# Seven half-size products for the fourth tile's second layer, with the sums of weights and one batch's copies of k moved

## The chip, the core and the metric

The kernel runs on one core of one Trainium2 chip. The core has a matrix engine (TensorE, PE in the profile, with PEld for its weight loads), a vector engine (VectorE, DVE), a scalar engine (ScalarE, ACT), GpSimd (POOL) and SyncE (SP). Each takes its instructions in the order in which they were written for it, and they wait for each other by semaphores. Here POOL and SP issue nearly all transfers. The metric is the device time of one execution in microseconds (us); the median of three runs stands for a kernel.

## The reference

Attention over 8 batches, 8 heads, 576 positions and head size 64, followed by a feed-forward network over all 4608 tokens. Heads 0 to 3 attend to the last 32 positions, heads 4 to 7 to every fourth of the last 128.

```python
scores = scale * np.matmul(q, k.transpose(0, 1, 3, 2))
scores = np.where(masks[None, :, :, :], scores, -1000000000.0)
attn = np.exp(scores - np.max(scores, axis=-1, keepdims=True))
attn = attn / (np.sum(attn, axis=-1, keepdims=True) + 1e-09)
x = np.matmul(attn, v)          # then (4608, 512): tokens by heads and head size
h = np.maximum(x @ w_in, 0.0)   # w_in 512 x 2048
out = h * h @ w_out             # w_out 2048 x 512
```

## The kernel before

**Tiles and groups.** The 4608 tokens are nine tiles of 512 (the first two are worked in halves). Each tile has 32 groups of PE work. Groups 0 to 15 are the first layer: one group makes 128 rows of h for 512 tokens, ACT applies the maximum with 0 (L1038) and DVE squares in place in `h2T` (L1041). Groups 16 to 31 are the second layer. Over the whole program the third tile has groups 64 to 95, the fourth 96 to 127, the fifth 128 to 159. A group's number sets everything: `WEIGH` and the list `steps` name groups, and after a group has been written for the engines, the work that names it follows, the sums of weights first.

**Attention between the groups.** The attention of a batch is not a stage of its own. At certain groups a *visit* puts some 100 to 140 small matmuls (L408) into PE's queue: scores of one pair of heads, and products with v and row sums of another. Before a visit, ACT makes the exponents (L773) and DVE masks them (L778) and adds where blocks overlap (L781, L790). After it ACT makes the reciprocal (L740 to L755) and DVE writes the normalised result to `xT`, the first layer's input (L758, L762), which also frees the banks of PSUM that the visit wrote. In the fourth tile the visits fall after groups 101, 111 and 119 and belong to the fifth batch; the last one also makes scores of the sixth.

**Copies.** q and k come through POOL's loads, are turned by SP's transposes into `planes`, and are copied into place on DVE: k into `kbd` by L379 (code K), the ends of the far heads' k by L390 (code R) and of q by L388 (code I).

**Two forms of the second layer.** Tiles below `FAST` use `g2`: 4 blocks of 128 tokens times 16 f, 64 matmuls of 512 columns (L1322). A block reads f in order, four to a group, so the last four f are wanted by the fourth group. From `FAST` on, the tile uses `g2_fast`: seven products in place of eight of the matrix cut in two by two (a Strassen-Winograd scheme), each 8 f times 2 blocks of tokens of 256 columns, 112 matmuls (L1282). It needs
- four sums of weights, `w_sum`, in two halves each: eight DVE operations of 128 x 1024 (`weigh`, L1438), made once. They lie in the memory that staged the third batch's q and k;
- sums of activations, `h_sum`: `add_up` (L1177) makes for each half of f four operations of 128 x 1024 out of the squared `h2T`. They lie in the memory that staged the fourth batch;
- sums of results: DVE adds products into `whole` (L1184) besides ACT's copies.

With `FAST` the first layer also runs in another order: unit u makes row block f = u // 2 + 8 (u % 2), so two units make one row block of each half of f, and DVE squares them in one operation of 2 x 512. For the last two units it squares singly.

**The order of the products** while attention still runs beside (`crowded`) is M1, half of M2, M6, the rest of M2, M5, a visit, then M7, M3, M4. M1 reads h of the first eight f for one half of the tokens, M2 of the last eight, M6 and M5 read sums.

Of the kernel before, what the change touches and what calls it, by code (L numbers as in the profile page):

```python
# [64 lines left out]
def kernel(  # L65
# [12 lines left out]
    DM, DFF = moe_w_in.shape  # L78
# [16 lines left out]
    NT = 512  # L95
    NTILES = NTOK // NT
    XB = 2
    FAST = 4
    WEIGH = (95, 95, 102, 103, 104, 118, 118, 127)
    WEIGH_IN = (18, 19, 20, 21, 22, 23, 195, 195)  # L100
    GATHER = (219, 220, 228, 232)
    PAIRED = 5
# [50 lines left out]
    HD = DM // 2  # L153
# [573 lines left out]
    def natural_step(b: int, code: str):  # L727
# [37 lines left out]
        else:  # L765
            g = int(code[2])
            second = g ^ ((b, e) in [(x, 1) for x in (NATURAL, *range(FAST + 1, B))])
            n = 384 if e >= NE // 2 else (448, 384)[g]
# [222 lines left out]
    def ffn_groups(tk0: int, nt: int):  # L991
# [3 lines left out]
        early = NT <= tk0 <= 3 * NT  # L995
        per = NT // nt
        at = tk0 // nt % per * nt
        h2 = h2T[:, :, at : at + nt]
        fast = tk0 >= FAST * NT
        kts = (2, 0, 3, 1) if tk0 > 3 * NT else (2, 3, 1, 0) if tk0 == 2 * NT else (0, 1, 2, 3) if tk0 == 0 else (2, 3, 0, 1)  # L1000
# [3 lines left out]
        over = g0 // gr != (g0 + nm - 1) // gr  # L1004
# [151 lines left out]
        sums_at = {7: (0, 4), 15: (4, 8)} if not mixed else {}  # L1156
        visited, crowded = (FAST <= tk0 // NT < x for x in (B - 1, B - 2))

# [20 lines left out]
        final = tk0 + nt == NTOK  # L1179
# [3 lines left out]
        def plus(to, one, two_):  # L1183
            nc.vector.tensor_tensor(out=to, in0=one, in1=two_, op=ALU.add)  # L1184

        def keep(m, c0, c1, n=2):

            parts = [(0, half, tk0 + RES * half), (half, half, tk0)] if over else [(0, P, tk0)]
            for x, k, row in parts:
                to = out[row : row + RES * k, :].rearrange("(p m) c -> p m c", m=RES)  # L1190
                nc.sync.dma_start(to[:, m : m + 2 * n - 1 : 2, c0:c1], whole[x : x + k, m : m + 2 * n - 1 : 2, c0:c1])

        def after(name):

            bank = {k: t[:, :, :] for k, t in cur.items()}
            if name == "M1":
                nc.scalar.copy(c11, bank["X"])
            elif crowded and name in ("M6", "M5"):
                nc.scalar.copy(c21 if name == "M6" else c12, bank["X"])
            elif crowded and name != "M2":  # L1200
                to, one, two_ = {"M7": (c22, "V", c12), "M3": (c12, "Q", c12), "M4": (c21, "V", c21)}[name]
                plus(to, bank[one], two_)
                if not over or name != "M7":
                    keep(int(name != "M3"), HD if name == "M7" else 0, HD if name == "M4" and not over else DM)
            elif name == "M5":
                nc.scalar.copy(c22, bank["Y"])
            elif name == "M6":
                nc.scalar.copy(c12, bank["X"])
                if final:
                    plus(c12, c12, c22)  # L1210
            elif name == "M3":
                plus(c12, bank["Y"], c12)
            elif name == "M7":
                plus(c22, bank["X"], c22)
                keep(1, HD, DM)
            elif name == "M2":
                plus(c11, bank["Z"], c11)
                if not crowded:
                    keep(0, 0, HD if final else DM)
            elif name == "M4":  # L1220
                nc.scalar.copy(c21, bank["X"])
                keep(1, 0, HD)
# [203 lines left out]
    def weigh(x):  # L1426

        y, f = divmod(x, 2)
        fs, gs = slice(4 * f, 4 * f + 4), slice(NF // 2 + 4 * f, NF // 2 + 4 * f + 4)
        b11, b12, b21, b22 = (w_out_sb[:, z, c : c + HD] for z in (fs, gs) for c in (0, HD))  # L1430
        to = [w[:, fs, :] for w in w_sum]
        order = (
            (to[0], b12, b11),
            (to[2], b22, b12),
            (to[1], b22, to[0]),
            (to[3], b21, to[1]),
        )
        nc.vector.tensor_tensor(out=order[y][0], in0=order[y][1], in1=order[y][2], op=ALU.subtract)  # L1438
# [79 lines left out]
    groups, steps = [], []  # L1518
# [20 lines left out]
    for b in range(NATURAL, B):  # L1539
        t = G * (b - 1)  # L1540
        early = b == NATURAL
        def visit(at, scs, pvs):
            steps.append((at, 2, b, "V0" + "/".join(",".join(f"{x}{y}" for x, y in z) for z in (scs, pvs))))
# [32 lines left out]
        else:  # L1576
            visit(t + 15, [(b, 3), (b, 1)], [(b, 0), (b, 2)][: 1 + (b >= PAIRED)])
            quick = b > FAST
            if not quick:
# [23 lines left out]
        for x, code in enumerate(("K00", "K01", "K10", "K11")):  # L1603
            if b < PAIRED:
                steps.append((start + 2 + x // 2 if early else t - 6 + x, 1, b, code))
            else:
                steps.append((t - 30 + x // 2 if b > PAIRED else t - 16 + x, 1 + 2 * (b == PAIRED), b, code + "0"))
                steps.append((t + 1 + x, 1, b, code + "1"))
        for x, code in enumerate(("Q01", "Q10")):
            if b < PAIRED:  # L1610
# [7 lines left out]
    for g, group in enumerate(groups):  # L1618
# [9 lines left out]
        group()  # L1628
        for x in [x for x in range(len(WEIGH)) if WEIGH[x] == g]:
            weigh(x)  # L1630
# [38 lines left out]
```

## Time and profile before

| What | Value |
|---|---|
| median of three runs | 286.48 us (286.25 to 286.54) |
| the profiled execution | 285.32 us |
| its span | 283.5 us |
| PE busy | 277.6 us, 98% of the span |
| DVE busy | 200.5 us, 71% |
| ACT busy | 190.9 us, 67% |
| POOL busy | 122.8 us, 43% |
| granted TensorE clock | 1.0 |

The span is the time from the first instruction to the last in the profiled execution; 1.8 us lie around it. A row of the timeline gives start and length in us from the start of the span, the engine, the line, the operation, what it writes and reads, the shapes, and how many instructions of one kind were merged. What stands in brackets is idle time of the engine ahead of the row and who ended it. A row of the chain gives start, length and what the time went to. Instructions on DVE overlap at their ends, so the distance between two starts says how long one holds the queue.

### The profile page before, as it was taken

How to read it: one execution, taken by the hardware profiler on the slowest of the kernel's cores; microseconds unless marked ns; L12 is line 12 of the kernel's file. 1: busy time of each engine (PE TensorE's matmuls, PEld its weight loads, DVE VectorE, ACT ScalarE, POOL GpSimd, SP SyncE). 2: the span in 40 equal slices, each digit the busy share in tenths (PEclk: the TensorE clock that was granted, in tenths of full speed). 3: DMA queues.
4: the chain of work that ended last, by engine and by line, in shares of the span. 5: the costliest groups of instructions: out<-in, count | busy, mean ns of one | idle time of the engine just before them, and what ended most of it. 6: DMA issues, size and time to landing. Idle time of an engine off the chain costs nothing.

```text
span 283.5 us, 8614 instructions
## 1 busy us (share of the span) xinstructions
PE 277.6 (98%) x3545; PEld 195.7 (69%) x3545; DVE 200.5 (71%) x482; ACT 190.9 (67%) x387; POOL 122.8 (43%) x208
## 2 busy tenths in 40 slices
PE   7899999999999999999999999999999999999995
PEld 6589746958755545555545787578757887899984
DVE  2686644664859766779649867987787679889752
ACT  6788726786856875697556875687568657776620
POOL 8686358663672976667285778900000000000000
PEclk9999999999999999999999999999999999999999
DMA  8999999999999999999999999910400030000314
GB/s 119 196 183 205 206 198 218 191 145 168 187 168 214 166 140 191 201 148 151 145 230 178 130 163 146 146 30 2 150 0 3 2 124 26 0 2 0 114 37 150
DMA packets 85607, 36.70 MB, mean 129 GB/s; under 512 B 53312, under 2 KB 81728, under 8 KB 85568
## 3 DMA queue, kind: packets, MB, share of 16 engines
q0 software_dynamic: 49056, 18.49, 60.4%
q1 hardware_dynamic: 36368, 17.55, 30.5%
q8 instruction: 28, 0.46, 0.7%
q14 instruction: 11, 0.09, 0.2%
q10 hardware_dynamic: 144, 0.10, 0.1%
HBM read 37.50 MB, written 9.44 MB: 166 GB/s over the span
## 4 chain that ended last, share of the span: by engine, by line
PE 93%; DMA 2%; DVE 1%; POOL 1%; issue 1%; ACT 1%; POOLq 0%
PE pf L1025 35%; PE pf L1282 22%; PE pf L1322 20%; PE pa L1077 4%; PE po L408 2%; DMA kb<-in_k_dram 2%; PE po L1077 2%; PE pf L408 2%; PE pa L408 2%; PE pd L1077 1%; PE pd L408 1%; PE pa L841 1%; DVE planes L374 1%; DVE h2T L1041 1%; PE pf L893 0%
## 5 line engine op out<-in xcount | busy, mean ns | idle before, releaser
L1025 PE MATMUL pf<-xT,w_in 128*128 128x512 bf16 (+1 forms) x608 | 107.9, 335 | 0.0
L1025 PEld LDWEIGHTS <-w_in 128*128 128x128 bf16 x608 | 67.2, 114 | 34.7 <-issue 0.3
L1038 ACT ACTIVATE h2T<-pf 128x512 bf16<-128x512 f32 x119 | 69.2, 601 | 27.0 <-PE pf L1025 26.8
L1041 DVE TENSOR_TENSOR h2T<-h2T 128x512 bf16<-128x512 bf16 (+1 forms) x95 | 45.3, 493 | 22.4 <-ACT h2T L1038 20.7
L1322 PE MATMUL pf<-w_out_sb,h2T 128*128 128x512 bf16 x256 | 57.3, 379 | 0.1
L361 POOL DMA_DIRECT2D vbd<-in_v_dram x80 | 43.1, 551 | 20.9 <-DMA qb<-in_q_dram 10.4
L1322 PEld LDWEIGHTS <-h2T 128*128 128x128 bf16 x256 | 24.3, 98 | 27.9
L1282 PEld LDWEIGHTS <-h2T 128*128 128x128 bf16 x256 | 24.5, 98 | 3.0
L1328 ACT COPY whole<-pf 128x512 f32<-128x512 f32 x14 | 8.2, 584 | 14.1 <-PE pf L1322 14.0
L755 ACT ACTIVATE rec<-rec 128x576 f32<-128x576 f32 x24 | 16.3, 692 | 0.5
L353 POOL DMA_DIRECT2D vbd<-in_v_dram x20 | 11.9, 608 | 10.3 <-DMA qb<-in_q_dram 4.5
L1184 DVE TENSOR_TENSOR whole<-pf,whole 128x512 f32<-128x512 f32 (+2 forms) x19 | 12.0, 631 | 6.2 <-PE pf L1282 5.3
L215 POOL DMA_DIRECT2D kb<-in_k_dram x19 | 13.1, 690 | 7.5 <-DMA w_in<-in_moe_w_in_dram 2.5
L237 POOL DMA_DIRECT2D vbd<-in_v_dram x16 | 11.0, 693 | 11.3 <-DMA kb<-in_k_dram 7.2
L1282 PE MATMUL pf<-w_out_sb,h2T 128*128 128x256 bf16 x128 | 15.8, 273 | 0.0
L1282 PE MATMUL pf<-kb,h2T 128*128 128x256 bf16 x128 | 15.8, 273 | 0.0
L1282 PE MATMUL pf<-qb,qb 128*128 128x256 bf16 x128 | 15.3, 273 | 0.0
L215 POOL DMA_DIRECT2D qb<-in_q_dram x19 | 13.4, 704 | 3.7 <-DMA vd<-in_v_dram 1.5
L773 ACT ACTIVATE pt<-pa 128x384 bf16<-128x384 f32 (+1 forms) x26 | 12.0, 497 | 4.0 <-DVE xT L762 3.4
L1282 PEld LDWEIGHTS <-qb 128*128 128x128 bf16 x128 | 12.5, 98 | 1.4
L347 POOL DMA_DIRECT2D vd<-in_v_dram x20 | 12.1, 617 | 1.7 <-PE pf L1025 1.0
L758 DVE TENSOR_TENSOR xT<-pf,rec 128x512 bf16<-128x512 f32 x11 | 7.6, 689 | 7.3 <-ACT rec L755 7.3
(221 smaller groups left out, 498.9 us busy)
## 6 DMA issues: line engine op xcount, KB each, us to landing
out_dram<-whole SPq DMA_DIRECT2D x21, 256.0 KB, 3.9
out_dram<-whole SPq DMA_DIRECT2D x18, 128.0 KB, 6.0
qb<-in_q_dram POOLq DMA_DIRECT2D x7, 320.0 KB, 7.6
kb<-in_k_dram POOLq DMA_DIRECT2D x7, 320.0 KB, 7.9
vd<-in_v_dram POOLq DMA_DIRECT2D x34, 64.0 KB, 6.2
w_out_sb<-in_moe_w_out_dram POOLq DMA_DIRECT2D x4, 512.0 KB, 12.8
qb<-in_q_dram POOLq DMA_DIRECT2D x6, 256.0 KB, 6.9
kb<-in_k_dram POOLq DMA_DIRECT2D x6, 256.0 KB, 7.8
```

What stands on the lines that cost most here:

```text
L215: nc.gpsimd.dma_start(t[p0 : p0 + n, part, h0:h1, :], src[b, h0:h1, t0 : t0 + RES * n, :].rearrange("h (p r) d -> p h (r d)", r=RES),)
L347: nc.gpsimd.dma_start(vds[b][rows, e, :, :], v[b, H // 2 + 2 * e + (hl ^ crossed(b, e + NE // 2)), 0:512, :].rearrange("(m p r) d -> p m ( ...
L361: nc.gpsimd.dma_start(v_rows[b % 2][p0 + 16 * r : p0 + 16 * r + 16, e, :, :], v[b, 2 * e + hl, :, :].rearrange("(i m r) d -> r m i d", r=R ...
L408: nc.tensor.matmul(out, lhs, rhs, start=begin, stop=True, skip_group_check=True)
L755: nc.scalar.activation(rec[:, :], rec[:, :], ACT.Exp, scale=-1.0)
L773: nc.scalar.activation(pt, sp[b, e][g][:, 0:n], ACT.Exp, scale=SCALE)
L1025: nc.tensor.matmul(to, w_in_sb[piece][:, kt, c0 : c0 + 509 : 4], rhs, start=(kt == kts[0] and x == 0), stop=(kt == kts[-1] and x == per - ...
L1038: nc.scalar.activation(hv, acc[u][:, :].rearrange("p (x n) -> p x n", x=per), ACT.Relu)
L1041: nc.vector.tensor_tensor(out=hv, in0=hv, in1=hv, op=ALU.mult)
L1077: nc.tensor.matmul(to[:, x, :].rearrange("p (r m) -> p r m", r=2), lhs(2 * d + x, k), rhs(k), start=x == k == 0 and name in ("M1", "M5", " ...
L1282: nc.tensor.matmul(cur[bank][:, i, y0:y1], lhs(f, i), rhs(f)[:, y0:y1], start=f == 0 and (piece or name in fresh and i == 0), stop=f == NF ...
L1322: nc.tensor.matmul(cur[m][:, c0:c1], h2[:, f, P * m : P * m + P], w_out_sb[:, f, c0:c1], start=(f == 0), stop=(f == NF - 1),)
```

## The change

It does four things.

1. `FAST` goes from 4 to 3: the fourth tile's second layer is made by the seven products too, with its eight sums of activations and its four sums of results, and its first layer runs in the other order with squares in pairs. The fifth batch's exponents and masks take the order that goes with it.
2. The eight sums of weights move from groups 95 to 127 to groups 61, 61, 62 (the end of the second tile) and 83, 83, 87, 87, 87 (the third).
3. The sixth batch's copies of k for the first pair of near heads move from groups 112 to 115, in the second layer of the fourth tile, to groups 108 and 109, in its first layer. Its copies of ends are already there.
4. Two conditions make the stores of the fourth tile's results fit the order of its products: M2 stores the left half, M3 the right.

```diff
-    FAST = 4
-    WEIGH = (95, 95, 102, 103, 104, 118, 118, 127)
+    FAST = 3
+    WEIGH = (61, 61, 62, 83, 83, 87, 87, 87)
...
                 if not over or name != "M7":
-                    keep(int(name != "M3"), HD if name == "M7" else 0, HD if name == "M4" and not over else DM)
+                    keep(int(name != "M3"), HD if name == "M7" or name == "M3" and early else 0, HD if name == "M4" and not over else DM)
...
                 plus(c11, bank["Z"], c11)
-                if not crowded:
-                    keep(0, 0, HD if final else DM)
+                if not crowded or early:
+                    keep(0, 0, HD if final or early else DM)
...
-                steps.append((t - 30 + x // 2 if b > PAIRED else t - 16 + x, 1 + 2 * (b == PAIRED), b, code + "0"))
+                steps.append((t - (30 if b > PAIRED else 20) + x // 2, 1, b, code + "0"))
```

DVE's queue in the second layer of the third tile, around groups 83 to 88: `qb_95` and `kb_96` hold the sums of weights, `kbd` the copies of k, `planes` what they are copied from.

```order
 L388 COPY planes<-planes 64x8x16 x2
-L390 COPY kbd<-planes 64x4x2x16 x2
+L1438 TENSOR_TENSOR kb_96<-w_out_sb 128x1024
+L1438 TENSOR_TENSOR qb_95<-w_out_sb,qb_95 128x1024
+L390 COPY kbd<-planes 64x4x2x16 x2
+L1438 TENSOR_TENSOR qb_95<-w_out_sb,qb_95 128x1024
+L1438 TENSOR_TENSOR kb_96<-w_out_sb,qb_95 128x1024 x2
 L758 TENSOR_TENSOR xT<-po,rec 128x4x128
```

Two sums now stand ahead of the last two copies of the fifth batch's ends, and three behind them.

DVE's queue in the first layer of the fourth tile, from the normalisation after group 101's visit to the masks of group 111's visit, before:

```order
L758 TENSOR_TENSOR xT<-po,rec 128x4x128
L762 TENSOR_TENSOR xT<-pa,rec 64x4x16 x2
L1041 TENSOR_TENSOR h2T<-h2T 128x512
L1438 TENSOR_TENSOR kb_96<-w_out_sb 128x1024
L1041 TENSOR_TENSOR h2T<-h2T 128x512
L1438 TENSOR_TENSOR qb_95<-w_out_sb,qb_95 128x1024
L778 TENSOR_TENSOR pt<-pt,mask_n 128x448
L1041 TENSOR_TENSOR h2T<-h2T 128x512 x2
L778 TENSOR_TENSOR pt<-pt,mask_n 128x384
L790 TENSOR_TENSOR kbd<-pt 128x128
```

And now, where `qb_99` and `kb_100` hold the sums of activations:

```order
L758 TENSOR_TENSOR xT<-po,rec 128x4x128
L762 TENSOR_TENSOR xT<-pa,rec 64x4x16 x2
L1041 TENSOR_TENSOR h2T<-h2T 128x2x512
L1177 TENSOR_TENSOR qb_99<-h2T 128x1024
L1177 TENSOR_TENSOR h2T<-h2T 128x8x128
L1177 TENSOR_TENSOR qb_99<-qb_99,h2T 128x1024
L1177 TENSOR_TENSOR kb_100<-h2T,qb_99 128x1024
L778 TENSOR_TENSOR pt<-pt,mask_n 128x448
L1041 TENSOR_TENSOR h2T<-h2T 128x2x512
L778 TENSOR_TENSOR pt<-pt,mask_n 128x384
L790 TENSOR_TENSOR kbd<-pt 128x128
```

Four sums of activations stand ahead of the masks where two sums of weights stood among them.

DVE's queue from there to the second sums of activations, now (before, the copies L379 stood behind group 111's masks and ahead of the second layer's sums of weights, and there were no L1177):

```order
L1041 TENSOR_TENSOR h2T<-h2T 128x2x512
L379 COPY kbd<-planes 64x4x5x16 x2
L1041 TENSOR_TENSOR h2T<-h2T 128x2x512
L390 COPY kbd<-planes 64x4x2x16 x2
L379 COPY kbd<-planes 64x4x4x16 x2
L1041 TENSOR_TENSOR h2T<-h2T 128x512
L390 COPY kbd<-planes 64x4x2x16 x2
L388 COPY planes<-planes 64x8x16
L1041 TENSOR_TENSOR h2T<-h2T 128x512
L1177 TENSOR_TENSOR qb_99<-h2T 128x1024
L1177 TENSOR_TENSOR qb_99<-qb_99,h2T 128x1024
L388 COPY planes<-planes 64x8x16
```

The four copies of k now lie between the last squares of the first layer, and the last two squares (units 14 and 15) come behind copies of ends. On PE, only the matmuls of the fourth tile differ: the same 64 of the first layer in another order, and 112 of L1282 for 64 of L1322.

## The prediction

> **What bounds the kernel now.** I read the page first, then the chain of work that ended last, then the fourth tile's stage against the fifth's, then the timeline of VectorE in that stage.
>
> ```profile
> span 283.5 us, 8614 instructions
> PE 277.6 (98%) x3545; PEld 195.7 (69%) x3545; DVE 200.5 (71%) x482; ACT 190.9 (67%) x387; POOL 122.8 (43%) x208
> PE 93%; DMA 2%; DVE 1%; POOL 1%; issue 1%; ACT 1%; POOLq 0%
> ```
>
> TensorE (PE) is the bound: 98% busy, 93% of the chain. A change gains only what it takes from PE's queue, and loses whatever makes that queue stand still. VectorE (DVE) is 71% busy on average, so what matters is where its work lies.
>
> ```profile
> 114.28:144.97 30.69, 30.69 (x351) 15.86 (x350) 22.50 (x65) 22.44 (x48) 19.89 (x36) 1.00 1.37 165
> 144.97:173.61 28.64, 28.64 (x382) 20.34 (x380) 22.70 (x56) 20.20 (x40) 20.17 (x36) 1.00 1.24 166
> ```
>
> These are the fourth and the fifth tile by stretches (length, then busy PE, weight loads, DVE, ACT, POOL). The fifth already has the seven products and is shorter. DVE is about as busy in both, 22.5 and 22.7 us.
>
> The chain in order of time (start, length, what) has the matmuls of both second layers:
>
> ```profile
> 120.12 8.76 PE pf L1025 x40
> 129.76 7.01 PE pf L1322 x32
> 136.77 0.15 PE po L408
> 137.96 7.01 PE pf L1322 x32
> 159.98 7.09 PE pf L1282 x64
> 168.26 5.35 PE pf L1282 x48
> ```
>
> **Part A, the seven products.** They remove 64 matmuls (7.01 + 7.01 = 14.02 us) and add 112 at the fifth tile's pace (7.09 + 5.35 = 12.44 us, 0.111 each). That lies wholly on PE: gain 1.6 us. One ACT copy of a result goes, which is off the path. The four stores stay four, with the same bytes, on SP.
>
> **Part B, sums of weights in the second and third tile.** All eight are on DVE. The first three stand ahead of a normalisation that waits for ACT:
>
> ```profile
> 83.31 0.69 DVE L758 TENSOR_TENSOR xT<-pf,rec 128x512 bf16<-128x512 f32 x1 [2.45 <-ACT rec L755]
> 106.39 0.51 DVE L388 COPY planes<-planes 64x128 bf16<-64x128 bf16 x2
> 106.72 0.65 DVE L390 COPY kbd<-planes 64x128 bf16<-64x128 bf16 x2
> 109.47 0.69 DVE L758 TENSOR_TENSOR xT<-po,rec 128x512 bf16<-128x512 f32 x1 [2.10 <-ACT rec L755]
> 113.32 1.29 DVE L1438 TENSOR_TENSOR qb<-w_out_sb 128x1024 bf16<-128x1024 bf16 x2
> 135.51 0.69 DVE L1438 TENSOR_TENSOR qb<-w_out_sb,qb 128x1024 bf16<-128x1024 bf16 x1
> ```
>
> Two sums take 1.29 us and one takes 0.69, so each holds the queue for about 0.61. Three are 1.9 us and fit into the idle 2.45 ahead of 83.31: cost nothing, with 0.5 us of cover. Without that cover their 1.9 us would delay the third tile's first layer.
>
> The other five are dearer. Two of them now stand ahead of the last two copies of L390, which write the fifth batch's k for the ends of its heads. Those copies ended at 106.72 + 0.65 = 107.37; they will end at 107.37 + 2 x 0.61 = 108.59. The matmuls that read them:
>
> ```profile
> 107.91 0.22 PE L408 MATMUL pa<-planes,kbd 64*64 64x64 bf16 x4
> ```
>
> PE reaches these four at 107.91 and has the whole second layer queued behind them. It stands still for 0.7 us. The last three sums end by 108.51 + 3 x 0.61 = 110.4 and push the normalisation from 109.47 by 1 us. That is hidden: its result is read by the fourth tile's first layer at 114.28 or later, and two sums at 113.32 go from that queue. B costs 0.7 us.
>
> The Trainium skill (VectorE: DVE Perf Modes, "The DRAIN you can't avoid") says that the next operation does not start until the pipe has emptied, with an exception for one that is not held. Taken strictly each sum would hold the queue for its 0.69, and B would be 0.8. The trace shows 0.61, and I go by that.
>
> **Part C, DVE ahead of the visit at 128.88.** DVE in the fourth tile is not late before 122. Then it works without a pause until 136.8:
>
> ```profile
> 123.27 0.68 DVE L758 TENSOR_TENSOR xT<-po,rec 128x512 bf16<-128x512 f32 x1
> 124.36 0.42 DVE L1041 TENSOR_TENSOR h2T<-h2T 128x512 bf16<-128x512 bf16 x1
> 126.25 0.38 DVE L778 TENSOR_TENSOR pt<-pt,mask_n 128x448 bf16<-128x448 bf16 x1
> 126.55 0.75 DVE L1041 TENSOR_TENSOR h2T<-h2T 128x512 bf16<-128x512 bf16 x2
> 127.60 0.34 DVE L790 TENSOR_TENSOR kbd<-pt 128x128 bf16<-128x128 bf16 x2
> 130.07 0.63 DVE L390 COPY kbd<-planes 64x128 bf16<-64x128 bf16 x2
> 130.73 0.19 DVE L388 COPY planes<-planes 64x128 bf16<-64x128 bf16 x1
> 131.62 0.66 DVE L778 TENSOR_TENSOR pt<-pt,mask_n 128x448 bf16<-128x448 bf16 x2
> 132.58 0.62 DVE L778 TENSOR_TENSOR pt<-pt,mask_f 128x384 bf16<-128x384 bf16 x2
> 133.23 0.23 DVE L781 TENSOR_TENSOR kbd<-pt 128x128 bf16<-128x128 bf16 x1
> 133.38 0.50 DVE L379 COPY kbd<-planes 64x320 bf16<-64x320 bf16 x2
> 135.02 0.46 DVE L379 COPY kbd<-planes 64x256 bf16<-64x256 bf16 x2
> 153.44 0.69 DVE L1041 TENSOR_TENSOR h2T<-h2T 128x1024 bf16<-128x1024 bf16 x1
> 154.16 0.69 DVE L1177 TENSOR_TENSOR qb<-h2T 128x1024 bf16<-128x1024 bf16 x1
> ...
> 156.83 2.22 DVE L1041 TENSOR_TENSOR h2T<-h2T 128x1024 bf16<-128x1024 bf16 x4
> ```
>
> The last three rows are the fifth tile's: from 153.44 to 156.83 lie one square of 1024 and four sums of activations (L1177), 3.39 us for five, 0.68 each on the mean and 0.72 where one feeds the next. The four squares after them take 2.22, so each holds the queue for (2.22 - 0.69) / 3 = 0.5 to 0.6.
>
> I lay the new order on these prices. The normalisation waits for ACT:
>
> ```profile
> 122.19 0.68 ACT L755 ACTIVATE rec<-rec 128x576 f32<-128x576 f32 x1
> ```
>
> Released at 122.9, 0.7 later with B, so it starts at 123.6. It and its two small ones take 124.36 - 123.27 = 1.1, the square and the four sums 3.4, a mask 0.3, a square 0.6, a mask 0.4, the pair of L790 0.3: the visit's operands are complete at 129.7. PE is there at 120.12 + 8.76 + 0.7 = 129.6 and reads them in its first 0.2 us. By these rows the stall is 0.1 to 0.2; every ACT operation behind which DVE waits could make it 0.6. I take 0.4.
>
> **Part D, the tail of the first product.** M1's 16 matmuls read f = 0 to 7, and f = 7 is squared as unit 14 of the first layer. From 129.65 the queue holds: a square 0.60, two copies of k (133.38 row) 0.53, a square 0.68, two L390 0.66, two copies of k (135.02 row) 0.49, then that square, 0.42: done at 133.1. PE starts M1 at 129.76 + 0.7 + 0.4 = 130.9 and wants f = 7 after 14 x 0.111, at 132.4. Stall 0.7 to 0.9; the four moved copies alone are 1.0 of it. Before, units 14 and 15 were wanted only by the fourth group of f, so the same lateness cost nothing. I take 0.8.
>
> **Part E, the next two products.** Unit 15's square follows after two L390 and an L388 (0.66 + 0.22 + 0.42): 134.3, against PE's 133.3 + 7 x 0.111 = 134.1: 0.2. Then two sums, 0.68 and 0.72, give M6's second half at 135.8. PE has M2's last and M6's first eight, 9 x 0.111 = 1.0, from 134.3 and stands at 135.3: 0.5. E costs 0.7.
>
> **Part F, the second visit.** From 135.8 PE has 8 + 8 + 16 matmuls (3.6 us) and arrives at 139.35. DVE from 135.7: L388 0.2, masks 0.7, L790 0.3, two sums 1.2, masks 0.65, L781 0.15; then the normalisation, which frees banks that this visit writes, ends at 139.5, its two small ones at 139.9, and the sum into the output that frees a pf bank (L1184) at 140.5. PE stands for 0.2 at the first and up to 1.2 in all; the visit's work between hides some 0.3. I take 0.9.
>
> After the visit the sums of weights no longer lie in DVE's queue, and the chain runs from the visit at 168.1 into the sixth tile without a stall under the same load, so I cost the rest at nothing.
>
> **The sum.** -1.6 + 0.7 + 0.4 + 0.8 + 0.7 + 0.9 = +1.9, and 0.1 for what else runs beside it: +2.0. The profiled execution took 285.3 (span 283.5 and 1.8 around); I expect 287.3 (span 285.5). The runs' median is 286.48, 1.2 above the profiled one, so the forecast of the median is **288.5**. From the ends: B 0.5 to 0.8, C 0 to 0.6, D 0.4 to 1.3, E 0.4 to 0.9, F 0.4 to 1.2. They are one lateness of one queue and move together: +0.1 to +3.2, with the ends of all five at once unlikely.
>
> **Rivals.** *VectorE keeps up (faster).* The place is DVE's queue from 123.6 to 139.5. If it finished each item 0.9 us earlier, C and E would go and D and F shrink to almost nothing, and B alone would stand against A: -0.9, 285.6. For it: DVE's busy time in the fifth tile, 22.7 of 28.64 us, holds the same sums without a stall. Against it: there the copies of k are done by 153.4, before the sums; here they lie between the squares. It decides if unit 14's square is done by 132.4. Chance 0.07.
>
> *Just about even.* Half the lateness in C to F and B at 0.5 give +0.3 or so, 286.8, inside 0.2% (0.57 us), which is about what a measurement of this kernel can tell from no change. Chance 0.07.
>
> *The moved copies are blocked.* POOL issues loads beside them:
>
> ```profile
> 131.94 3.19 POOL L361 DMA_DIRECT2D vbd<-in_v_dram x6
> 147.97 1.21 DVE L379 COPY kbd<-planes 64x320 bf16<-64x320 bf16 x4
> ```
>
> If each of the four moved copies waited for one issue (3.19 / 6 = 0.53), D would grow by 2.1 and the time be 290.6. For it: in the fifth tile four copies took 1.21 instead of 1.0 us. Against it: the pair at 133.38 took 0.50 while POOL was issuing. Chance 0.07 for the whole, and 0.15 for some 0.5 of it (289.0, inside the forecast's range). The Trainium skill (SBUF — State Buffer, "SBUF: two separate sides") has this rule: VectorE in a two-port mode and GpSimd lock each other out for a whole instruction. The row at 133.38 does not show it.
>
> That the change doesn't take effect is excluded by the order of instructions: 112 products stand where 64 stood.
>
> The forecast as described, 287.2 to 290.0, has 0.79. Slower by over 0.2%: 0.86; within: 0.07; faster: 0.07. The range 287.2 to 290.0 leaves out the faster and even cases and the full blocking.
>
> **What will show it.** Right: the stage between the two tiles' first matmuls grows from 30.69 to about 32; a hole of 0.7 before the matmuls of L408 that read kbd near 108; holes in the seven products after M1's fourteenth matmul, in M6, and at the second visit, each released by DVE; a second layer of 12.4 us apart from its holes. Wrong: no DVE-released holes in that stage (then 285.6), copies L379 over 0.4 us each (then higher), or new holes after 147, which I have at nothing.

## The result, and the profile after

The changed kernel took 288.73 us (median of 4 executions, 288.22 to 288.97) against 286.43 us for the kernel before beside it (286.25 to 286.54): a ratio of 1.0078, 95% interval 1.0061 to 1.0096, or 2.3 us slower. The forecast was 288.5, slower, in the range 287.2 to 290.0. Ratios here and below leave out single executions more than 1.5% above the fastest of their kernel.

The profiled execution of the changed kernel took 288.72 us, as its median. That of the kernel before had been 1.2 us under its own median. So the two traces lie further apart than the medians: the executions by 3.4 us, their spans (286.67 and 283.54) by 3.1. What follows accounts for the 3.1 of the spans; why the medians lie only 2.3 apart, two traces do not show.

The page's span and busy times, and the shares of the chain that ended last:

```profile
span 286.7 us, 8706 instructions
PE 277.1 (97%) x3583; PEld 201.0 (70%) x3593; DVE 207.4 (72%) x487; ACT 190.7 (67%) x386; POOL 122.6 (43%) x208
PE 84%; DVE 7%; ACT 3%; DMA 2%; issue 2%; POOL 1%; DVEq 0%; POOLq 0%
```

TensorE has 0.5 us less work on record than before, and the kernel is longer all the same. (Ten matmuls are missing from the record of the changed kernel: 3583 stand beside 3593 weight loads, of which each matmul has one.) VectorE's share of the chain went from 1% to 7%. The fourth tile and the fifth, by stretches (length, then busy PE, weight loads, DVE, ACT, POOL):

```profile
115.23:148.04 32.81, 30.49 (x400) 20.76 (x398) 25.02 (x62) 22.69 (x48) 21.34 (x38) 1.00 1.39 162
148.04:176.75 28.71, 28.71 (x381) 20.43 (x380) 23.36 (x58) 19.64 (x39) 20.52 (x36) 1.00 1.26 163
```

The fourth tile's stretch grew from 30.69 to 32.81 us, and TensorE now idles there. The fifth is what it was. TensorE's waits between 80 and 150 us (who waits for whom, total, times, longest). In this stretch of the kernel before the same view lists none. The two of L1322 are matmuls missing from the record (the weight loads there show no wait):

```profile
PE pf L1282 <- DVE h2T L1041: 1.4, 2, 1.1
PE pa L408 <- DVE kbd L390: 0.9, 1, 0.9
PE po L408 <- DMA vbd<-in_v_dram: 0.3, 1, 0.3
PE pf L1322 <- issue: 0.3, 2, 0.2
PE pf L1282 <- DVE qb L1177: 0.3, 1, 0.3
PE pf L408 <- DVE whole L1184: 0.2, 1, 0.2
```

Here an idle time counts from the modelled end of the matmul before. What a stop costs is the distance between two starts less the usual 0.111, some 0.15 us more. The same stops in TensorE's timeline:

```profile
130.75 1.70 PE L1282 MATMUL pf<-w_out_sb,h2T 128*128 128x256 bf16 x14
133.52 1.16 PE L1282 MATMUL pf<-w_out_sb,h2T 128*128 128x256 bf16 x9 [1.07 <-DVE h2T L1041]
134.99 0.28 PE L1282 MATMUL pf<-w_out_sb,h2T 128*128 128x256 bf16 x1 [0.31 <-DVE h2T L1041]
136.44 1.05 PE L1282 MATMUL pf<-qb,qb 128*128 128x256 bf16 x8 [0.30 <-DVE qb L1177]
140.46 0.39 PE L408 MATMUL po<-pt,vbd 64*64 64x96 bf16 x2 [0.35 <-DMA vbd<-in_v_dram]
```

The 14 matmuls at 130.75 are M1's first fourteen; the fifteenth waits for f = 7. Next come M2's last and the second half of M6. The last row is the second visit: it is put down to a load, but the normalisation that frees its bank had ended only at 140.40, 0.06 us earlier; in experiment 4 the same row is put down to the normalisation. VectorE's timeline beside it, with rows left out:

```profile
131.53 0.90 DVE L390 COPY kbd<-planes 64x128 bf16<-64x128 bf16 x2
132.44 0.57 DVE L379 COPY kbd<-planes 64x256 bf16<-64x256 bf16 x2
133.04 0.42 DVE L1041 TENSOR_TENSOR h2T<-h2T 128x512 bf16<-128x512 bf16 x1
134.51 0.42 DVE L1041 TENSOR_TENSOR h2T<-h2T 128x512 bf16<-128x512 bf16 x1
134.97 0.69 DVE L1177 TENSOR_TENSOR qb<-h2T 128x1024 bf16<-128x1024 bf16 x1
135.69 0.69 DVE L1177 TENSOR_TENSOR qb<-qb,h2T 128x1024 bf16<-128x1024 bf16 x1
139.71 0.69 DVE L758 TENSOR_TENSOR xT<-po,rec 128x512 bf16<-128x512 f32 x1
140.81 0.69 DVE L1184 TENSOR_TENSOR whole<-pf,whole 128x512 f32<-128x512 f32 x1
```

The stop at 133.52 ends just behind unit 14's square (133.46), the one at 134.99 behind unit 15's (134.93), the one at 136.44 behind the second sum (136.38), the one at 140.46 behind the normalisation (140.40). VectorE did not pause between 131.53 and 141.50.

### The profile page after: what moved, and what is told of

Same layout as the page of the kernel before. It is cut to its first block, busy times and chain, and to the rows that moved or that the text cites. A ratio compares the mean times of both kernels' runs of the same rounds, so it can differ in the third digit from the quotient of the medians.

```text
span 286.7 us, 8706 instructions
## 1 busy us (share of the span) xinstructions
PE 277.1 (97%) x3583; PEld 201.0 (70%) x3593; DVE 207.4 (72%) x487; ACT 190.7 (67%) x386; POOL 122.6 (43%) x208
## 4 chain that ended last, share of the span: by engine, by line
PE 84%; DVE 7%; ACT 3%; DMA 2%; issue 2%; POOL 1%; DVEq 0%; POOLq 0%
PE pf L1025 34%; PE pf L1282 23%; PE pf L1322 12%; PE pa L1077 4%; DMA kb<-in_k_dram 2%; PE po L1077 2%; PE po L408 2%; PE pf L408 2%; PE pa L408 1%; DVE h2T L1041 1%; DVE qb L1177 1%; PE pd L1077 1%; DVE kbd L390 1%; PE pa L841 1%; DVE xT L758 1%
## 5 line engine op out<-in xcount | busy, mean ns | idle before, releaser
L1041 DVE TENSOR_TENSOR h2T<-h2T 128x512 bf16<-128x512 bf16 (+1 forms) x88 | 44.7, 520 | 20.3 <-ACT h2T L1038 18.5
L1322 PE MATMUL pf<-w_out_sb,h2T 128*128 128x512 bf16 x182 | 41.9, 379 | 1.0 <-issue 0.6
L1282 PEld LDWEIGHTS <-h2T 128*128 128x128 bf16 x320 | 30.6, 98 | 5.6 <-DVE h2T L1041 1.9
L1322 PEld LDWEIGHTS <-h2T 128*128 128x128 bf16 x192 | 18.2, 98 | 20.8
L1282 PE MATMUL pf<-w_out_sb,h2T 128*128 128x256 bf16 x160 | 20.0, 273 | 1.4 <-DVE h2T L1041 1.4
L1184 DVE TENSOR_TENSOR whole<-pf,whole 128x512 f32<-128x512 f32 (+2 forms) x23 | 14.8, 641 | 7.9 <-PE pf L1282 7.1
L1282 PE MATMUL pf<-kb,h2T 128*128 128x256 bf16 x160 | 19.6, 273 | 0.0
L1282 PE MATMUL pf<-qb,qb 128*128 128x256 bf16 x160 | 19.3, 273 | 0.3 <-DVE qb L1177 0.3
L1282 PEld LDWEIGHTS <-qb 128*128 128x128 bf16 x160 | 15.6, 98 | 2.3 <-DVE qb L1177 0.6
L1328 ACT COPY whole<-pf 128x512 f32<-128x512 f32 x10 | 5.8, 585 | 9.0 <-PE pf L1322 8.9
L758 DVE TENSOR_TENSOR xT<-po,rec 128x512 bf16<-128x512 f32 x13 | 8.9, 688 | 3.9 <-ACT rec L755 3.8
```

Of the source, the lines that this page charges most:

```text
L1041: nc.vector.tensor_tensor(out=hv, in0=hv, in1=hv, op=ALU.mult)
L1282: nc.tensor.matmul(cur[bank][:, i, y0:y1], lhs(f, i), rhs(f)[:, y0:y1], start=f == 0 and (piece or name in fresh and i == 0), stop=f == NF ...
L1322: nc.tensor.matmul(cur[m][:, c0:c1], h2[:, f, P * m : P * m + P], w_out_sb[:, f, c0:c1], start=(f == 0), stop=(f == NF - 1),)
```

## The experiments

These ran on four chips, beside the kernel before (median 285.38 to 285.54 there). Executions of one kernel scatter by 1 to 3 us. In the traces of all but 12, the same weight load near 75 us starts between 74.8 and 77.3, and from there to the third tile's last visit they agree to 0.1 us; so the scatter lies ahead of it, where loads still arrive. So each is read by its ratio with its interval and by its trace between 107 and 148 us. That part splits into four, each from a start to the next: the end of the third tile (from its last visit, near 107, to the fourth tile's first layer; 7.05 us before, 8.18 after), the first products (from the fourth tile's first product to its second visit), the second visit (to the next product), and the last products (to the fifth tile).

| kernel | ratio to before | 95% interval | third tile's end | first products | second visit | last products |
|---|---|---|---|---|---|---|
| before | 1 | | 7.05 | 7.01 | 1.19 | 6.92 |
| after | 1.0078 | 1.0061–1.0096 | 8.18 | 9.71 | 2.16 | 5.25 |
| 1: sums behind copies | 1.0049 | 1.0024–1.0074 | 7.05 | 9.57 | 1.91 | 5.25 |
| 2: sums early, alone | 1.0043 | 1.0017–1.0068 | 8.37 | 7.01 | 1.19 | 6.92 |
| 3: no sums of activations | 1.0036 | 1.0009–1.0063 | 8.08 | 7.25 | 3.84 | 5.25 |
| 4: copies of k back | 1.0079 | 1.0052–1.0106 | 8.64 | 9.24 | 1.91 | 5.25 |
| 5: as 3, 36 fewer on PE | 1.0017 | 0.9990–1.0043 | 8.09 | 7.26 | 1.38 | 5.27 |
| 6: copies on ScalarE | 1.0046 | 1.0019–1.0074 | 7.05 | 7.56 | 3.52 | 5.25 |
| 7: as 6, 36 fewer on PE | 1.0044 | 1.0025–1.0064 | 7.05 | 7.56 | 1.87 | 5.57 |
| 8: before, 36 fewer | 1.0031 | 1.0007–1.0054 | 7.05 | 7.01 | 1.19 | 6.91 |
| 9: copies split | 1.0024 | 1.0002–1.0046 | 7.06 | 7.49 | 2.12 | 5.25 |
| 10: as 9, 24 more on PE | 0.9993 | 0.9974–1.0012 | 7.05 | 7.48 | 1.91 | 5.25 |
| 11: before, 24 more | 1.0026 | 1.0006–1.0047 | 7.05 | 7.01 | 1.19 | 6.92 |
| 12: as 9, 12 more on PE | 1.0062 | 1.0009–1.0115 | 7.06 | 7.60 | 1.91 | 5.25 |

### 1 and 2: the sums of weights

The first puts the last five sums behind the copies that TensorE waits for; the second makes the new times of the sums alone, in the kernel before.

```diff
 # 1, in the kernel after
-    WEIGH = (61, 61, 62, 83, 83, 87, 87, 87)
+    WEIGH = (61, 61, 62, 87, 87, 87, 87, 87)
 # 2, in the kernel before
-    WEIGH = (95, 95, 102, 103, 104, 118, 118, 127)
+    WEIGH = (61, 61, 62, 83, 83, 87, 87, 87)
```

> The changed kernel with the two sums of weights of group 83 moved to group 87, behind the last two copies of ends (L390). If the hole of 1.1 us before the matmuls that read these copies is real loss, it goes whole and nothing takes its place, since the normalisation behind the sums has over 4 us until it is read: 288.7 - 1.1 = 287.6 us. If the time is set by DVE's lateness in the fourth tile alone and a start later by 1.1 us was merely waited for elsewhere, nothing changes: 288.7.

> The kernel before with only the new groups of the sums of weights. By my account they cost PE the hole of 0.7 to 1.1 us at the copies of ends and save PE nothing: 286.4 + 0.9 = 287.3 us. If taking six sums out of DVE's queue in the fourth tile were worth something to the kernel before, part of it would come back: 286.4 to 286.8.

In the first the third tile's end is back at 7.05 and the fourth tile keeps its stops. In the second the stop stands alone, and nothing after it moved. Its row in TensorE's timeline:

```profile
109.84 0.22 PE L408 MATMUL pa<-planes,kbd 64*64 64x64 bf16 x3 [1.11 <-DVE kbd L390]
```

Part B is this stop and nothing else: 1.13 us of the changed kernel's trace, 1.32 of the second's, 1.2 us by the second's ratio (0.0043 x 285.5), about 0.9 by the first's against the fourth's (1.0079 - 1.0049 = 0.0030), which has B and whose copies make little difference, as below.

### 3: without the sums of activations

The fourth tile's eight sums are left out; products that read sums read one plain quarter of the activations instead. This kernel leaves out work that the result needs.

```diff
-            for to, one, two_, op in (todo[x] for x in which):
+            for to, one, two_, op in (todo[x] for x in which if not early):
...
-            return lambda f, i: (h_sum_last if final else h_sum)[x][:, f, P * i : P * i + P]
+            return raw(0, 0) if early else lambda f, i: (h_sum_last if final else h_sum)[x][:, f, P * i : P * i + P]
```

> The changed kernel without the eight sums of activations (L1177) of the fourth tile; three of its products read plain h in their place, with the same shapes. This leaves 5.3 us out of DVE's queue and nothing out of PE's. If lateness of DVE's queue makes the holes of the second layer (1.2 after M1's fourteenth matmul, 0.9 in M2 and M6, about 0.7 at the second visit), these shrink to 0.3 us or less and the time is 288.7 - 2.6 = 286.1 us. If the holes come from the banks, from POOL's loads or from PE's own change of order, they stay: 288 us or more.

With 5 us less on VectorE the stops D and E are gone: the first 64 products take 7.25 us, 0.16 over their 7.09. But the time fell by 0.4% and not by the 0.9% I had expected, since a new stop took their place at the end of the second visit:

```profile
141.84 0.27 PE L408 MATMUL pf<-pt,ones 64*64 64x192 bf16 x1 [2.26 <-issue]
```

The releaser "issue" means that TensorE waited for nothing that the profile shows. Every operand was there.

### 4: the copies of k back

```diff
-                steps.append((t - (30 if b > PAIRED else 20) + x // 2, 1, b, code + "0"))
+                steps.append((t - 30 + x // 2 if b > PAIRED else t - 16 + x, 1 + 2 * (b == PAIRED), b, code + "0"))
```

> The changed kernel with the sixth batch's first copies of k back in groups 112 to 115, behind the squares and the sums. They were 1.0 us of the 1.2 us hole at M1's fifteenth matmul. That hole shrinks to 0.2, but the same 1.0 us now stand in the queue ahead of the second visit's masks, whose hole grows by as much: 288.7 us again, within 0.3. If the copies were blocked where they stand now, or if the move of the copies was what cost the time, it is 287.7 or less.

The ratio is that of the changed kernel, as expected. The stop at f = 7 (D) vanished, those at unit 15 and the second sum (E) stayed, and the second visit's first grew from 0.35 to 1.21:

```profile
135.61 0.28 PE L1282 MATMUL pf<-w_out_sb,h2T 128*128 128x256 bf16 x1 [0.18 <-DVE h2T L1041]
137.06 1.05 PE L1282 MATMUL pf<-qb,qb 128*128 128x256 bf16 x8 [0.30 <-DVE qb L1177]
141.94 0.39 PE L408 MATMUL po<-pt,vbd 64*64 64x96 bf16 x2 [1.21 <-DVE xT L758]
```

So 0.86 of D's 1.23 us came back one stop later. From the first product to the fifth tile the fourth experiment takes 16.40 us, the changed kernel 17.12, of which 0.3 is the late piece told below. The ratio did not fall with it, but this trace has a longer end of the third tile (8.64 against 8.18), where a pair of L388 took 1.03 us and not 0.58. So moving the copies within VectorE's queue moved most of the stop. VectorE's backlog is close to one amount, and TensorE pays it at whatever it needs next.

### 5 to 8: what held the second visit, and the copies on ScalarE

The changed kernel has 3,593 matmuls and as many weight loads (the page of 3 lists them all), 7,186 instructions. The profile lists a DMA queue named "instruction" (q8) with 28 packets of 0.02 MB, one every 256 of these or so. Counted in such steps, a border falls 16 instructions before the end of the fourth tile's second visit, where the new stop was. The kernel's opening gives a way to move it without touching the visit: it holds 28 matmuls of 183 columns that only keep TensorE busy until the first loads are there.

```diff
 # 5 (in 3), 7 (in 6), 8 (in the kernel before): 36 instructions fewer
-    ... L1:v0dp s28x183 T00 ...
+    ... L1:v0dp s10x512 T00 ...
 # 6 and 7, in 1: the sixth batch's copies of ends (R) and of k (K) on ScalarE
-            steps.append((at + x // 2 * (b != PAIRED - 1) + x * (b == PAIRED - 1), 1, b, code))
+            steps.append((at + x // 2 * (b != PAIRED - 1) + x * (b == PAIRED - 1), 1, b, code + "a" * (b == PAIRED)))
...
-                steps.append((t - (30 if b > PAIRED else 20) + x // 2, 1, b, code + "0"))
+                steps.append((t - (30 if b > PAIRED else 20) + x // 2, 1, b, code + "0" + "a" * (b == PAIRED)))
```

> The third experiment again (the changed kernel with the fourth tile's eight sums of activations left out, its products reading plain halves instead), with one thing more: the 28 matmuls of 183 columns that open the kernel while it waits for its first loads are 10 of 512 columns, the same columns in 36 instructions fewer on TensorE. Everything behind them stands 36 places earlier in TensorE's program, unchanged. Theory: the hole of 2.5 us that appeared at the end of the fourth tile's second visit, with nothing waited for, is TensorE's next piece of program arriving late. The pieces have 256 instructions, and a border of two pieces lies 16 instructions before the end of that visit, which runs through its 204 instructions in 1.2 us. With 36 instructions fewer the border lies ten products behind the visit, and those ten take 1.1 us: no hole at the end of the visit, at most 1.3 us about ten matmuls later, and a time 1 to 2.5 us below the third experiment's, ratio to the kernel before 0.995 to 1.000. Rival: the hole is a wait for the transposed q and k or for an eviction, which no count of instructions moves: the same hole before the same matmuls, ratio about 1.0036 as there.

> The first experiment again (the last five sums of weights behind the copies of k) and, with it, the sixth batch's four copies of k and its eight copies for the ends of heads on ScalarE instead of VectorE; the same work. Theory of VectorE's queue: in the fourth tile's second layer this takes some 2 us from the queue that was late by 1.2 us at the tail of the first product, 0.9 in the next two and 0.7 at the visit: these holes shrink to 1 us or less together, and with the hole near 108 gone the ratio to the kernel before is 0.997 to 1.000. If ScalarE, which now copies between its activations, is as late with what it evicts, the holes come back with ScalarE as the releaser, and the ratio stays at 1.004 or above. If the program of TensorE arrives late at the end of the second visit, as the theory of the run beside this one has it, a hole of 1 to 2.5 us stands there with nothing waited for, and the ratio is 1.001 to 1.005.

> The run before this one with the 36 instructions fewer at TensorE's start. If both theories hold (VectorE's queue makes the holes of the fourth tile, and the late piece of program the one at the end of its second visit), nearly all of the 1.6 us of the seven products remains: ratio to the kernel before 0.994 to 0.998, and no hole over 0.5 us in the fourth tile. If only the queue matters, as the run before this one. If neither, 1.004 or above.

> The kernel before with the 36 instructions fewer at TensorE's start and nothing else: a control. In that kernel the borders between pieces of 256 instructions lie early or in the middle of the visits of the fourth and later tiles, and stay in or before them when moved by 36, so no gain there. Theory: ratio 1.000, within 0.2 %; at most 0.5 us less, if the hole of 0.56 us near 14 us, which also has nothing waited for, is such a border too and moves to where TensorE waits anyway. If the opening matmuls themselves matter (the clock, or the end of the opening), the time of all runs with this edit moves with it, and this run gives by how much.

The stop went with the border. In 5 the second visit takes 1.38 us instead of 3.84, and no other part of the tile changed. In 6 the stop is there, in 7 it is gone from the visit, for the same work; 0.4 us of it stand ten products behind the visit (last products 5.57), where the border now lies. TensorE's timeline in 6, then in 7, at the visit:

```profile
130.71 2.78 PE L1282 MATMUL pf<-w_out_sb,h2T 128*128 128x256 bf16 x24 [0.77 <-ACT h2T L1038]
141.57 0.27 PE L408 MATMUL pf<-pt,ones 64*64 64x192 bf16 x1 [1.46 <-issue]
```

```profile
132.06 2.78 PE L1282 MATMUL pf<-w_out_sb,h2T 128*128 128x256 bf16 x24 [0.86 <-ACT h2T L1038]
140.68 0.19 PE L408 MATMUL pf<-pt,vbd 64*64 64x64 bf16 x1 [0.22 <-DVE whole L1184]
```

The ratios had been expected at 1.000 or less for 5 and 0.998 or less for 7; both came out higher. That of 5 fell by 0.5 us where the visit got 2.5 shorter, and that of 7 not at all. The control, 8, says a part of why: the same edit made the kernel before 0.9 us slower. The rest, 1.0 us in 5 and 0.4 in 7, is within the intervals. The opening has a border too. In the kernel before (first row) TensorE stops there for 0.56 us near 14 us, with nothing waited for; moved 36 instructions on, it stops for 1.96 us ahead of the first layer (second row, from 8):

```profile
13.99 0.45 PE L893 MATMUL pf<-planes 64*64 64x32 bf16 x15 [0.56 <-issue]
```

```profile
15.86 1.06 PE L1025 MATMUL pf<-xT,w_in 128*128 128x256 bf16 x8 [1.96 <-DVE pt L904]
```

The second is put down to VectorE, which was not the cause by the clock alone: the mask that it names ended at 16.1. The packet of the queue named "instruction" began at 11.58 us in the first and at 13.51 in the second, took 0.9 and 1.0, and TensorE went on 1.5 and 1.4 us after its end. At the second visit it was the same:

| kernel | packet, start to end | TensorE goes on | after the packet's end | stop |
|---|---|---|---|---|
| after | 140.06–141.03 | 142.40 | 1.4 | 0.31 |
| 3 | 138.79–140.43 | 141.84 | 1.4 | 2.5 |
| 6 | 139.06–140.00 | 141.57 | 1.6 | 1.7 |
| 7 | 140.19–141.46 | 142.90 | 1.4 | 0.4 |
| 9 | 139.08–140.05 | 141.49 | 1.4 | 0.27 |
| 10 | 133.31–134.56 | | | none |

(The stop is the distance between starts; the idle time in the rows is some 0.2 shorter.)

The count of instructions is the same at each of the two places, whatever work stands there. The view by stretches, from the start to just ahead of the stop, has the number of weight loads in its second bracket (the kernel before, 8, and 3):

```profile
0.00:13.98 13.98, 11.62 (x223) 8.80 (x223) 6.38 (x21) 10.30 (x21) 10.67 (x20) 1.00 1.08 157
0.00:15.85 15.85, 12.24 (x223) 6.91 (x223) 8.02 (x26) 12.00 (x24) 11.47 (x21) 1.00 1.11 164
0.00:141.83 141.83, 135.86 (x2003) 91.04 (x2003) 91.49 (x245) 99.01 (x212) 88.77 (x147) 1.00 1.39 175
```

The opening's stop has 223 weight loads ahead of it in both, though 8 has done 18 fewer of the opening's. The later one has 2,003 in all five kernels of the table that have it, also in 7, where other work stands at that count. Between the two lie 1,780 weight loads, as many matmuls and 24 semaphore instructions that the trace lists for TensorE: 3,584, or 14 times 256.

The new stop in 6 and 7 is one of ScalarE, 0.8 us at the first product: two copies of k took it 0.82 us ahead of an activation of the first layer. On VectorE they take 0.5.

### 9 to 12: the copies split, and a longer opening

Of the four copies of k only the first two go to ScalarE, which was the late one in 6. The openings of 10, 11 and 12 have more instructions, so that the border lies earlier.

```diff
 # 9, 10 and 12, in 1, with the line for R as in 6
-                steps.append((t - (30 if b > PAIRED else 20) + x // 2, 1, b, code + "0"))
+                steps.append((t - (30 if b > PAIRED else 20) + x // 2, 1, b, code + "0" + "a" * (b == PAIRED and x < 2)))
 # 10 (in 9) and 11 (in the kernel before); 12 (in 9) has s34x110
-    ... L1:v0dp s28x183 T00 ...
+    ... L1:v0dp s40x128 T00 ...
```

> The copies split: as in the sixth experiment the last five sums of weights stand behind the copies of k and the eight copies for the ends of heads are on ScalarE, but of the sixth batch's four copies of k only the first two are; the other two go back to VectorE. In the sixth experiment ScalarE was late with an h2T of the first layer (a hole of 0.77 us, released by it) behind two copies of k that took it 0.82 us, while VectorE stood idle for 0.48 and 0.96 us. Theory: that hole goes, and the one with nothing waited for at the end of the second visit stays, at 1 to 2 us, since the program of TensorE has the same length: ratio to the kernel before 1.000 to 1.004.

> The run before this one with a longer program ahead: the opening's 28 matmuls of 183 columns are 40 of 128, the same columns in 24 instructions more, so that the border of two pieces lies 24 instructions earlier in the second visit, and the instructions at which TensorE asks for the next piece come twelve products (1.3 us) earlier. Theory of the late piece: the hole at the end of the second visit shrinks by some 1.1 us, to 0.4 or less, and the opening's hole of 0.56 us near 14 us moves by 24 instructions and stays about as long. With no other hole over 0.3 us in the fourth tile the seven products show: ratio to the kernel before 0.995 to 0.999. If the opening with 40 matmuls is slower by itself, the next run gives by how much. Rival (the visit's hole is a wait for data): it stays, and the ratio is that of the run before.

> The kernel before with the 40 opening matmuls of 128 columns and nothing else, as the control of the run before this one: ratio 1.000 within 0.25 %, with what differs lying ahead of 17 us.

> The copies split as in the ninth experiment, with an opening of 34 matmuls of 110 columns in place of 28 of 183: 12 instructions more, at the same length (40 of 128 took 4.39 us, 0.11 each, where 28 of 183 took 3.79; 34 should take 3.8). The border of two pieces lies 12 instructions earlier in the second visit, and TensorE comes to the asking place six products (0.7 us) earlier than in the ninth, at no cost in the opening. Theory: ratio to the kernel before 0.995 to 1.000, no hole with nothing waited for in the fourth tile over 0.5 us. If the small scatter of the loads in the first 60 us covers it, 0.998 to 1.002. If it is slower than 1.002, the opening's count of instructions matters in another way than by its length.

In 9 and 10 the stops of D and E are gone, and the third tile's end is as before. One stop over 0.15 us is left in the fourth tile of 10, at its second visit:

```profile
138.62 0.19 PE L408 MATMUL pf<-pt,vbd 64*64 64x64 bf16 x1 [0.22 <-DVE whole L1184]
```

I had expected the second visit of 9 to stop for 1 to 2 us at the border; it stopped for 0.27, since TensorE came there later than in 6 by the clock, and the packet did not. The tenth is the fastest version with seven products in the fourth tile: 0.9993, not told apart from the kernel before (0.995 to 0.999 had been expected), against 1.0078 for the change as made. The control with its opening, 11, was 0.26% slower than the kernel before. That is not the opening's cost alone, since the trace of 11 has a late piece of its own, in the fifth tile, by the same count three steps of 256 instructions behind the border at 2,003 weight loads:

```profile
174.17 0.83 PE L1282 MATMUL pf<-w_out_sb,kb 128*128 128x256 bf16 x6 [0.64 <-issue]
```

So what the tenth would gain with a better opening is not shown by the ratios. The part of the tenth's trace from the fourth tile's first visit to the fifth tile took 15.63 us, and 16.00 in the kernel before. So 0.37 of the 1.58 us of the seven products came through. The rest is 0.4 in the first products and 0.7 in the second visit, in stops of 0.2 to 0.4 behind VectorE's normalisation and its sum into the output, and 0.1 in the first visit.

The twelfth was to have that shift at no cost in the opening, and was slower: 1.0062 from five executions, with a wide interval, where 1.000 or less was expected. Its profile does not explain the ratio, since the execution profiled took 290.14 us, the longest of six, and is not among the five, whose granted clock was 0.994 to 1.0. In it the 34 matmuls took 3.2 us and not the 3.8 expected, TensorE then stood for 1.06 us waiting for the first k, and its clock fell in the second and third of the page's 40 slices (granted clock in tenths, each slice 7.2 us):

```profile
PEclk9579999999999999999999999999999999999999
5.87 0.31 PE L841 MATMUL pa<-mk,kb 64*64 64x64 bf16 x8 [1.06 <-DMA kb<-in_k_dram]
7.20:14.40 7.20, 7.20 (x109) 4.14 (x110) 3.40 (x9) 3.30 (x11) 4.51 (x7) 0.52 1.34 190
```

No other trace of this study shows a granted clock under 0.9 in any slice, and this one does not say that the wait made it fall. Its fourth tile reads as that of 9. Why the twelfth is slower, and whether its shift would gain with another opening, stays open.

## Why the prediction was right

The direction, the engine and the places were as forecast, and nothing after 147 us moved. The time was right by more than the working deserved. Against the profiled span the sum was +2.0 and the spans show +3.1: four of the five losses were 0.2 to 0.5 us larger than forecast, and one 0.3 smaller. The forecast of the median added 1.2 for the distance of the kernel before's profiled execution to its median, and the changed kernel's trace has no such distance. The two errors nearly cancel, and that is luck. The range does not follow from the working either: the ends of the five losses, +0.1 to +3.2, give 286.6 to 289.7.

| part | forecast | measured | how |
|---|---|---|---|
| A, the seven products | -1.6 | -1.58 | 14.02 to 7.09 + 5.35 |
| B, sums ahead of L390 | 0.7 (0.5 to 0.8) | 1.13 | third tile's end, 8.18 - 7.05 |
| C, first visit | 0.4 (0 to 0.6) | 0.1 | 0.99 - 0.88 |
| D, f = 7 | 0.8 (0.4 to 1.3) | 1.23 | 1.34 between starts - 0.11 |
| E, M2 and M6 | 0.7 (0.4 to 0.9) | 0.93 | 0.47 + 0.46 |
| F, second visit | 0.9 (0.4 to 1.2) | 1.43 | 9.71 - 7.09 - 1.23 - 0.93 = 0.46, and 2.16 - 1.19 = 0.97 |

The measured parts add up to +3.2; the rest of the spans differs by 0.1 the other way.

**B** failed in its size, and left its range. The step was "each holds the queue for about 0.61", taken from sums that follow each other. In their new place the first follows copies and the second is followed by copies:

```profile
106.25 0.58 DVE L388 COPY planes<-planes 64x128 bf16<-64x128 bf16 x2
106.86 0.69 DVE L1438 TENSOR_TENSOR kb<-w_out_sb 128x1024 bf16<-128x1024 bf16 x1
107.47 0.68 DVE L1438 TENSOR_TENSOR qb<-w_out_sb,qb 128x1024 bf16<-128x1024 bf16 x1
108.19 0.62 DVE L390 COPY kbd<-planes 64x128 bf16<-64x128 bf16 x2
108.86 0.22 PE L408 MATMUL pa<-planes,kbd 64*64 64x64 bf16 x3 [0.93 <-DVE kbd L390]
```

Before, L390 had begun 0.18 us ahead of the end of L388. Now a copy and a sum next to each other do not overlap: 0.03 and 0.04 us lie between. That is some 0.2 at the first hand-over and 0.11 at the second (0.72 for a sum instead of 0.61). From the start of L388 to the end of the copies it took 2.56 us where 2.20 was forecast, so the copies ended at 108.81 and not at 108.59, although L388 had begun 0.14 earlier. TensorE had come 0.17 earlier by the same clock. The Trainium skill (VectorE: DVE Perf Modes, "Two Vector instructions with no wait between them") says that an instruction is held until those ahead have finished when an input of it starts in another quarter of the partitions than the last one read, or its output in another than the last one written. The copies read and write halves of the partitions and the sums all of them, so the rows agree with it as far as they go. The rule that the prediction weighed, of 0.69 for each, would have given 0.8, nearer but for another reason: two sums in a row still start 0.61 apart.

**C** was all but nothing. The last operands of the visit ended at 129.88 and TensorE came at 129.76; only its last reads were late.

**D, E** went as forecast, by the mechanism named. Unit 14's square was done at 133.46 where 133.1 was forecast, since the pair of L390 at 131.53 took 0.90 us and not 0.66, beside a load of POOL, as below. In 3, without the sums, and in 9 and 10, with the copies elsewhere, both stops are gone; in 4, which puts back only the four moved copies, D is gone and most of its time turns up in F. That D's cause was "the four moved copies" is thus true of the place and not of the cost: the cost is the backlog, of which the eight sums are 5 us.

**F** was larger for two reasons. The queue was 0.6 later from E on (second sum done at 136.38, forecast 135.8), and it gave TensorE its bank at 140.40 instead of 139.5. And 0.31 of the 1.43 is the late piece of program, which the forecast did not have. VectorE's delay hid the rest of it: the kernel without the sums met it in full.

Of the rivals, *VectorE keeps up* fails by its own sign: unit 14's square was wanted by 132.4 and done at 133.46. *The moved copies are blocked* did not come about for the moved copies: the four took 1.05 us in two pairs while POOL issued loads, against 1.0 before. It did for the copies of L390 between them, which the prediction had left out. The pair at 131.53, one copy at a time, and POOL's issue beside it:

```profile
131.53 0.58 DVE L390 COPY kbd<-planes 64x128 bf16<-64x128 bf16 x1
132.12 0.30 DVE L390 COPY kbd<-planes 64x128 bf16<-64x128 bf16 x1
131.23 0.75 POOL L215 DMA_DIRECT2D kb<-in_k_dram  x1
```

The first copy took 0.28 us more than the second and ended 0.13 us after the issue. That is part of D.

## What to carry to other kernels

Price an operation in a queue by what stands next to it in the new order, not only by its own rows: a hand-over between unlike operations cost 0.1 to 0.2 us more here, at the one spot where TensorE waited. When one engine is late as a whole, moving single operations within its queue mostly moves the stop (4); work taken off the engine (3), or given to one with room (9, 10), removed the stops here. And before blaming data for a stop with no releaser, count instructions.

## What the runs showed that was not expected

TensorE's program arrives in pieces, and a piece can be late. The stops with nothing waited for, near 14 us and at the end of the second visit, moved or vanished when only the number of earlier instructions changed. They kept their place in the count of instructions, and ended 1.4 to 1.6 us after a packet of the queue named "instruction" had ended. A visit runs through 204 instructions in 1.2 us, where the same number in products takes 11 us, so a border late in a visit leaves little time for the next piece. A change of 96 instructions, as this one, also decides where in the later visits the borders fall. What makes TensorE ask for a piece was not settled: counted from the start of the visit, the packet came 3.7 us earlier in 10 than in 9, for 24 instructions.

A copy on VectorE can be held by a load that POOL is issuing, and the traces show when. In the fourteen of them, 96 single copies of L390 had no issue of POOL beside them and took 0.29 to 0.32 us. Of 192 beside one, 40 took over 0.33, up to 0.62. Each of the 40 had begun at least 0.24 us into an issue and ended 0.10 to 0.15 us after that issue; of those that began earlier none was held. No run was made to test this, and a change in VectorE's order by some tenths decides which copies are hit.

In the profiled execution of 12, one alone, the granted clock was 0.52 from 7.2 to 14.4 us, behind waits of 0.22 and 1.06 us between small matmuls. The Trainium skill (TensorE: Matmul & The Clock Gate, "What's actually happening") puts the fall behind an idle window of about 3.4 us; no single wait here was that long, and what made the clock fall stays open.
